# One addition of the last four variances to VectorE, and GpSimd's small operations of rows 8 to 13 in the order of rows

## The chip, the cores and the metric

The kernel runs on one core of a Trainium2 chip. The metric is the device time of one execution in microseconds (us): the median of several runs. The core's engines are named as the profile names them: PE (TensorE), DVE (VectorE), ACT (ScalarE), POOL (GpSimd) and SP (SyncE).

## The reference

Two blocks follow each other, each with a residual connection, on `x` of 2048 tokens by 448 channels. The first is a long convolution that is gated by the normalised input; the second is an MLP that mixes the tokens.

```python
def _layernorm(x, axis=-1, eps=1e-5):
    m = jnp.mean(x, axis=axis, keepdims=True)
    v = jnp.var(x, axis=axis, keepdims=True)
    return (x - m) / jnp.sqrt(v + eps)
...
    h = x + _A_ref(_layernorm(x, axis=-1), A_k, A_v, A_shift_k, A_ssm_k, A_ssm_D)   # q * (causal conv of kv + kv * D)
    h2 = h + _B_ref(_layernorm(h, axis=-1), B_w1, B_b1, B_w2, B_b2)
...
    u = _gelu(jnp.einsum("bsd,sf->bdf", h, w1) + b1)      # inside _B_ref, h normalised
    y = jnp.einsum("bdf,fs->bds", u, w2) + b2
```

## The kernel before, in words

The 2048 tokens lie as 128 partitions times 16 rows (token = 16 * partition + row). "Row r" below is one tile of 128 partitions by 448 channels. The convolution is done by a transform in two stages each way (`k1`, `k2`, `u1`, `u2`, products and `i1`, and at last `i2`); then the MLP's first matmuls (`mlp`) sum over the 16 rows.

**The stretch around the change** is the end of the convolution and the beginning of the MLP. For each row r:

- PE makes two matmuls for the row (line 1310) in a PSUM bank.
- From row 4 on, ACT (line 1320) or DVE (line 1322, rows 4, 14 and 15) reads the bank, scales it by the row's `qs[:, r, 3]` (one over the deviation of x's row) and adds 1. This is called the gate here.
- DVE multiplies with `x - mean` (line 1330 for rows 4 to 15), which gives the row of `h`, and leaves the row's sum in an accumulator. This is called the combination.
- ACT squares the row (line 1358) and accumulates the sum of squares.
- For each pair of rows POOL makes mean, square of the mean, variance, variance plus epsilon, and the power of -0.5: lines 1368, 1371, 1373, 1378 and 1382, five small operations on 128x2 numbers.
- DVE writes the normalised row into `Q` (line 1389). This is called the norm.
- PE multiplies row r of `Q` with row r of the first seven blocks of `w1` (line 1436, seven matmuls for a row, `mlp.r`).

**Statistics of x** are made before that, by DVE with `bn_stats` and `bn_aggr` (lines 1238 and 1240), and POOL adds epsilon (line 1246) and takes the power (line 1249) for four rows at once. For the last four, rows 12 to 15, these two are the steps `q.8:4` (the addition) and `q.8:5` (the power). The last aggregate that they need is `q.7:1`, of row 12.

**The order of work** on each engine is written out by hand in `ORDER`, a list of steps for each engine; an engine does its list strictly in order, and waits by semaphores for what other engines, or its own earlier instructions, have made. The steps that the text speaks of, by rows:

| rows | line 1368 | 1371 | 1373 | 1378 | 1382 (power) | norms on DVE |
|---|---|---|---|---|---|---|
| 4, 5 | i2.36:0 | i2.36:1 | i2.36:2 | i2.37 | i2.38 | i2.39, i2.40 |
| 6, 7 | i2.49:0 | i2.49:1 | i2.49:2 | i2.50 | i2.51 | i2.52, i2.53 |
| 8, 9 | i2.62:0 | i2.62:1 | i2.62:2 | i2.63 | i2.64 | i2.65, i2.66 |
| 10, 11 | i2.75:0 | i2.75:1 | i2.75:2 | i2.76 | i2.77 | i2.78, i2.79 |
| 12, 13 | i2.88:0 | i2.88:1 | i2.88:2 | i2.89 | i2.90 | i2.91, i2.92 |

DVE's list around the change: `q.7:1` (aggregate of row 12), norm of row 4, combination of 8, norm of 5, combinations of 9 and 10, norms of 6 and 7, combinations of 11, 13 and 12, norms of 8 and 9, gate of 14, norms of 10 and 11, combination of 14, gate of 15. PE's list: ... `mlp.7`, then parts of `mlp.8` to `mlp.11` mixed: the first matmul after `mlp.7` needs row 8 of `Q`, the fifth row 9, the eleventh row 10; then come the two matmuls of row 15 (line 1310), and then the first that needs row 11.

Of the kernel before, what the change touches and what calls it, by code (L numbers as in the profile page):

```python
# [80 lines left out]
    ),  # L81
# [118 lines left out]
class _Sched:  # L200
# [50 lines left out]
    def op(self, W, fn, r=(), w=(), br=(), bw=(), n=0, kind=None, est=None, dmab=None, keng=16, rate=None, after=(), safter=(), mode=0):  # L251
        if (self.tag, self.t0) != self.step:
            self.step = (self.tag, self.t0)
            self.count[self.tag] = self.count.get(self.tag, -1) + 1
        o = _Op()
        o.id = len(self.ops)
        o.engs = W if isinstance(W, tuple) else (W,)
        o.eng = None
        o.fn = fn
        o.is_dma = dmab is not None  # L260
        o.nbytes = dmab or 0
        o.keng = keng
        o.lat = 2000.0 + o.nbytes / (22.0 * keng) if o.is_dma else 0.0
        if o.is_dma:
            o.est = {e: (585.0 if e == "pool" else 700.0 if keng <= 8 else 460.0) for e in o.engs}
        elif est is not None:
            o.est = dict(est) if isinstance(est, dict) else {e: est for e in o.engs}
        else:
            o.est = {e: self.est_of(e, n, kind) for e in o.engs}
        o.ev = None  # L270
        o.mode = mode
        o.step = "%s.%d" % (self.tag, self.count[self.tag])
        o.rate = rate or (208.0 if keng == 8 else 425.0)
        o.tag = self.tag
        o.acq = []
        o.bufs = []
        o.extra = []
        preds = set(after)
        spreds = set(safter)
        for spec in r:  # L280
            for c in self._cells(spec):
                preds.update(c.w)
                c.r.append(o.id)
        for spec in w:
            g = spec[2] if len(spec) > 2 else None
            for c in self._cells(spec):
                rd = [x for x in c.r if x != o.id]
                if g is not None and c.g == g and not rd:
                    preds.update(c.gb)
                    c.w.append(o.id)  # L290
                else:
                    base = rd if rd else list(c.w)
                    preds.update(base)
                    c.w = [o.id]
                    c.r = []
                    c.g = g
                    c.gb = base
        for b in br:
            if len(self.ops) and all(self.ops[x].engs == ("pe",) for x in b.writers):
                preds.add(b.writers[-1])  # L300
            else:
                preds.update(b.writers)
            b.readers.append(o.id)
            o.bufs.append(b)
            b.users.append(o.id)
        for b in bw:
            if not b.writers:
                o.acq.append(b)
            else:
                spreds.add(b.writers[-1])  # L310
            b.writers.append(o.id)
            o.bufs.append(b)
            b.users.append(o.id)
        preds.discard(o.id)
        spreds -= preds
        o.preds = sorted(preds)
        o.spreds = sorted(spreds)
        self.ops.append(o)
        return o.id
# [259 lines left out]
def _build(nc, A_q, A_k, A_v, A_shift_k, A_ssm_k, A_ssm_D, B_w1, B_b1, B_w2, B_b2, out):  # L579
# [54 lines left out]
    with ctx:  # L634
        sch = _Sched(nc, ctx, n_dma_sems=112, small_off=SMALL)
        op = sch.op
# [5 lines left out]
        def view(off, shape, dtype=bf16):  # L642
            size = 4 if dtype in (f32, i32) else 2
            n = 1
            for s_ in shape:
                n *= s_
            ap = AR[:, off // 2: off // 2 + n * size // 2]
            if dtype is not bf16:
                ap = ap.bitcast(dtype)
            if len(shape) == 2:  # L650
                ap = ap.rearrange("p (a b) -> p a b", b=shape[1])
            elif len(shape) == 3:
                ap = ap.rearrange("p (a b c) -> p a b c", b=shape[1], c=shape[2])
            return ap
# [48 lines left out]
        def small(nb):  # L703
            o = sm["o"]
            sm["o"] = o + nb
            assert sm["o"] <= TOT
            return o
# [511 lines left out]
        o_qst = small(16 * 16)  # L1219
# [7 lines left out]
        def emit_q():  # L1227
            op("pool", lambda e, W: e.memset(cst[:, 0:2], -0.5), w=[(o_c2, 16, "c")])
            op("pool", lambda e, W: e.memset(cst[:, 2:3], 1.0), w=[(o_c2, 16, "c")])
            sch.t0 = T_Q  # L1230
            qs = view(o_qst, [R, 4], f32)
            for g in range(8):
                sch.t0 = T_Q + T_DQ * g
                for i in range(2):
                    r = 2 * g + i
                    ob = o_bst + 24 * (r % 4)
                    bs = view(ob, [6], f32)
                    op("dve", lambda e, W, bs=bs, r=r: e.bn_stats(out=bs, in_=XR(r)), r=[(oX(r), DB)],  # L1238
                       w=[(ob, 24)], n=D, kind="1x")
                    op("dve", lambda e, W, bs=bs, r=r: e.bn_aggr(out=qs[:, r, 0:2], in_=bs), r=[(ob, 24)],  # L1240
                       w=[(o_qst + 16 * r, 8)], n=6)
                if g >= 2 and g % 2 == 0:
                    continue
                r0, nr = (2 * g, 2) if g < 2 else (2 * g - 2, 4)
                rs = [(o_qst + 16 * (r0 + i), 16) for i in range(nr)]
                op("pool", lambda e, W, r0=r0, nr=nr: e.tensor_scalar(
                    out=qs[:, r0:r0 + nr, 2], in0=qs[:, r0:r0 + nr, 1], scalar1=EPS, scalar2=None, op0=ALU.add),
                   est=500.0, r=rs, w=[(o_qst + 16 * (r0 + i) + 8, 4) for i in range(nr)])
                op("pool", lambda e, W, r0=r0, nr=nr: e.tensor_tensor(
                    out=qs[:, r0:r0 + nr, 3], in0=qs[:, r0:r0 + nr, 2], in1=cst[:, 0:1].broadcast_to([128, nr]), op=ALU.pow),  # L1250
                   est=1000.0, r=rs + [(o_c2, 16)], w=[(o_qst + 16 * (r0 + i) + 12, 4) for i in range(nr)])
# [178 lines left out]
        def emit_mlp():  # L1430
# [21 lines left out]
            for r in range(R):  # L1452
# [23 lines left out]
                ("k1", emit_stage1, (KT, o_KT, TK, o_TK, "k")), ("k2", emit_stage2, (TK, o_TK, 1.0 / 2048.0)),  # L1476
                ("u1", emit_stage1, (V, o_V, TU, o_TU, "u")),  
                ("xload", emit_xload, ()), ("bias", emit_bias, ()), ("q", emit_q, ()),
                ("u2", emit_stage2, (TU, o_TU, None)), ("ew", emit_ew, ()), ("i1", emit_products_i1, ()), ("ct", emit_ct, (True,)), ("xn", emit_xn, ()), ("w1a", emit_w1_load, (0,)),
                ("warm", emit_warm, (N_WZ, T_I2 - 50.0, lambda: i1_last[-1:])),  # L1480
# [40 lines left out]
```

## Time and profile before

| | before |
|---|---|
| median of 3 runs | 172.8 us (172.39 to 172.85) |
| the profiled execution | 172.45 us, of which the profile's span is 170.3 us |
| PE busy | 160.4 us, 94% of the span |
| DVE busy | 104.0 us, 61% |
| ACT busy | 88.4 us, 52% |
| POOL busy | 61.2 us, 36% |
| granted clock of PE | 1.0 in this execution |

Times in the rows of the trace count from the start of the span. In a row of the timeline the columns are the start, the duration, the engine, the line and operation, and in brackets the idle time of the engine before it with what ended it. On DVE and PE the recorded duration of an instruction reaches somewhat beyond the start of the next one, since they are pipelined.

### The profile page before, as it was taken

To read this page: it belongs to the slowest core of one execution; us is meant where nothing else is said; L and a number is where in the kernel's file an instruction comes from. 1 tells how busy PE (TensorE), PEld (TensorE's weight loads), DVE (VectorE), ACT (ScalarE), POOL (GpSimd) and SP (SyncE) were. 2 spreads that over 40 slices of the span, in tenths; PEclk is the share of its full clock that TensorE was granted. 3 is DMA by queue.
4 is the path that set the end of the run, shared out by engine and by line. 5 is a ranking of instruction groups with operands and counts; after the bars stand their busy time and mean duration, and the time that the engine had idled before them with its cause. 6 is when DMAs were issued, how large, how long until landed. Compare 5 with 4: busy or idle time off the path is not lost.

```text
span 170.3 us, 3575 instructions
## 1 busy us (share of the span) xinstructions
PE 160.4 (94%) x1419; PEld 93.5 (55%) x1419; DVE 104.0 (61%) x192; ACT 88.4 (52%) x128; POOL 61.2 (36%) x156
## 2 busy tenths in 40 slices
PE   6999999899988899969998999999999999999994
PEld 2786756324333343524554555555567777777783
DVE  7998998999999999999977730000003223132231
ACT  3597859779989999998976143102360000000000
POOL 8346727482870554685888540000000000000000
PEclk9999999999999999999999999999999999999999
DMA  5999898775648875657999999930000111101111
GB/s 163 416 304 383 276 293 344 283 287 192 211 118 295 284 208 156 188 171 250 390 394 402 422 421 422 416 127 0 0 0 4 54 54 54 54 0 58 54 54 54
DMA packets 15564, 35.15 MB, mean 206 GB/s; under 512 B 3804, under 2 KB 9644, under 8 KB 15548
## 3 DMA queue, kind: packets, MB, share of 16 engines
q1 hardware_dynamic: 12396, 28.26, 45.6%
q0 software_dynamic: 3008, 6.58, 12.0%
q8 instruction: 11, 0.18, 0.4%
q10 hardware_dynamic: 144, 0.08, 0.2%
q14 instruction: 5, 0.04, 0.1%
HBM read 22.05 MB, written 1.84 MB: 140 GB/s over the span
## 4 chain that ended last, share of the span: by engine, by line
PE 60%; DVE 12%; ACT 11%; POOL 7%; DMA 6%; issue 3%; DVEq 0%; POOLq 0%; ACTq 0%
PE ps L1458 25%; PE ps L1446 12%; ACT arena L739 7%; PE ps L1436 6%; DMA arena<-arena 6%; PE ps L1025 3%; PE ps L966 3%; DVE arena L1161 3%; PE ps L1178 2%; PE ps L1038 2%; ACT arena L1069 2%; PE ps L1059 2%; DVE arena L1007 2%; POOL arena L1075 2%; DVE arena L1340 2%
## 5 line engine op out<-in xcount | busy, mean ns | idle before, releaser
L1461 DVE SCALAR_TENSOR_TENSOR arena<-ps,arena 128x448 bf16<-128x448 f32 (+2 forms) x17 | 11.1, 656 | 55.9 <-PE ps L1458 55.9
L1458 PE MATMUL ps<-arena 128*128 128x448 bf16 (+2 forms) x238 | 42.7, 342 | 0.0
L1458 PEld LDWEIGHTS ps<-arena 128*128 128x128 bf16 x238 | 33.3, 145 | 9.5
L1436 PE MATMUL ps<-arena 128*128 128x448 bf16 x112 | 23.8, 353 | 0.6 <-DVE arena L1389 0.6
L739 ACT CAST arena<-ps 128x896 bf16<-128x896 f32 (+1 forms) x29 | 23.3, 897 | 0.7 <-PE ps L1178 0.4
L1069 ACT CAST arena<-ps 128x896 bf16<-128x896 f32 x24 | 20.3, 915 | 5.2 <-PE ps L1059 5.2
L1446 PE MATMUL ps<-arena 128*128 128x448 bf16 x112 | 22.5, 352 | 0.0
L1075 POOL DMA_DIRECT2D arena<-arena x32 | 17.6, 555 | 12.9 <-ACT arena L1069 12.8
L1426 ACT ACTIVATE arena<-ps,arena 128x448 bf16<-128x448 f32 x14 | 7.9, 642 | 18.2 <-PE ps L1436 10.6
L1436 PEld LDWEIGHTS ps<-arena 128*128 128x128 bf16 x112 | 10.7, 98 | 11.4 <-DVE arena L1389 1.7
L1161 DVE TENSOR_TENSOR arena<-arena 128x1792 bf16<-128x1792 bf16 x16 | 16.6, 1080 | 0.2
L1446 PEld LDWEIGHTS ps<-arena 128*128 128x128 bf16 x112 | 11.0, 98 | 10.2
L1059 PE MATMUL ps<-arena 128*32 128x448 bf16 x256 | 15.0, 355 | 1.7 <-ACT arena L1069 0.5
L1094 PE MATMUL ps<-arena 128*64 128x448 bf16 x128 | 15.3, 360 | 1.0 <-ACT arena L740 0.4
L1178 PE MATMUL ps<-arena 64*128 64x448 bf16 x128 | 14.2, 351 | 1.4 <-ACT arena L739 0.6
L1202 POOL DMA_DIRECT2D arena<-arena x16 | 9.3, 587 | 12.7 <-ACT arena L739 12.7
L1358 ACT ACTIVATE arena<-arena 128x448 bf16<-128x448 f32 x14 | 8.0, 573 | 6.3 <-DVE arena L1330 6.2
L1094 PEld LDWEIGHTS ps<-arena 128*64 128x64 f16 x128 | 5.5, 108 | 10.1 <-ACT arena L739 2.8
L1178 PEld LDWEIGHTS ps<-arena 64*128 64x128 f16 x128 | 5.3, 94 | 9.6 <-DVE arena L1161 3.5
L1059 PEld LDWEIGHTS ps<-arena 128*32 128x32 f16 x256 | 5.4, 95 | 9.2 <-ACT arena L1069 2.1
L1389 DVE TENSOR_SCALAR arena<-arena 128x448 bf16<-128x448 f32 x16 | 7.8, 510 | 4.0 <-POOL arena L1382 4.0
L1238 DVE BATCH_NORM_STATS2 arena<-arena 128x6 f32<-128x448 bf16 x16 | 9.6, 609 | 0.0
(97 smaller groups left out, 193.7 us busy)
## 6 DMA issues: line engine op xcount, KB each, us to landing
arena<-in_B_w_dram SPq DMA_DIRECT2D x8, 896.0 KB, 10.1
arena<-in_B_w_dram SPq DMA_DIRECT2D x2, 2048.0 KB, 17.1
arena<-arena SPq DMA_DIRECT2D x16, 224.0 KB, 3.7
arena<-arena POOLq DMA_DIRECT2D x32, 112.0 KB, 3.8
arena<-in_B_w_dram SPq DMA_DIRECT2D x2, 1536.0 KB, 19.0
arena<-arena POOLq DMA_DIRECT2D x13, 196.0 KB, 4.1
arena<-in_A_k_dram SPq DMA_DIRECT2D x4, 448.0 KB, 5.9
arena<-in_A_v_dram SPq DMA_DIRECT2D x4, 448.0 KB, 9.1
```

The costliest lines, as they stand in the source:

```text
L739: return e.copy(out=dst(), in_=src())
L1059: op("pe", lambda e, W, b=b, r=r, q=q, x=x, c0=c0: e.matmul(PS[32 * q:32 * q + 32, b.slots[x], 0:D], E[:, 2 * r + x, c0:c0 + 32], src[:, r ...
L1069: return e.copy(out=dst, in_=Ppair(b)) if W == "act" else e.tensor_copy(out=dst, in_=Ppair(b))
L1075: shuf[tag].append(op(q_, lambda e, W, g=g, i=i, a=a, nu=nu, jh=jh: e.dma_start(T[a + i:a + i + 4 * nu - 3:4].rearrange("p (j k) c d -> p ...
L1094: op("pe", lambda e, W, b=bs[h], h=h, j=j, c=c, par=par: e.matmul(PS[64 * par:64 * par + 64, b.slots[c], 0:D], FW[:, 64 * c:64 * c + 64], ...
L1161: op("dve", lambda e, W, m=m, i=i: e.tensor_tensor(out=MR(m.slots[0]).rearrange("p (x y) d -> p x y d", x=2), in0=TU[:, i].unsqueeze(2).br ...
L1178: k = op("pe", lambda e, W, b=bs[h], m=ms[h], par=par, t=t, tab=tab, xy=xy, P=P: e.matmul(Pb(b, par), tab[P, :], MR(m.slots[0])[P, xy, :], ...
L1238: op("dve", lambda e, W, bs=bs, r=r: e.bn_stats(out=bs, in_=XR(r)), r=[(oX(r), DB)], w=[(ob, 24)], n=D, kind="1x")
L1436: op("pe", lambda e, W, r=r, fc=fc, b=bs[fc]: e.matmul(Pb(b), W1A[:, r, 128 * fc:128 * fc + 128], Q[:, r, :], start=(r == 0), stop=(r == R ...
L1446: op("pe", lambda e, W, r=r, fc=fc, b=b: e.matmul(Pb(b), W1B[:, r, 128 * (fc - n0):128 * (fc - n0) + 128], Q[:, r, :], start=(r == 0), sto ...
L1458: op("pe", lambda e, W, r=r, fc=fc, b=b, d0=d0, d1=d1: e.matmul(Pb(b)[:, d0:d1], W2[fc // 7][:, fc % 7, r:S:R], G[:, fc, d0:d1], start=(fc ...
L1461: op("dve", lambda e, W, r=r, b=b, A=A, d0=d0, d1=d1: e.scalar_tensor_tensor(out=XR(r)[:, d0:d1], in0=Pb(b)[:, d0:d1], scalar=bm[:, r:r + ...
```

## The change

The addition `q.8:4` (line 1246, 128x4 numbers of rows 12 to 15) is done by DVE, right after the aggregate `q.7:1` that it needs and ahead of the norm of row 4; POOL had done it between the powers `i2.38` and `q.8:5`. In POOL's list the operations of rows 8 to 13 stand in the order of rows: the power of rows 8 and 9 (`i2.64`) comes ahead of the first two operations of rows 10 and 11 (`i2.75:0`, `i2.75:1`), and the first one of rows 12 and 13 (`i2.88:0`) behind the power of rows 10 and 11 (`i2.77`). The sum of the means and the bias (`i2.0`, line 1287) stays ahead of `i2.89`. Nothing else moves.

```diff
 "dve":
-        "i2.29:0 i2.16:0 i2.30:0 i2.47:0 i2.26:0 i2.43:0 q.7:0 q.7:3 i2.27:0 q.7:1 i2.39:0 i2.56:0 i2.40:0 "
+        "i2.29:0 i2.16:0 i2.30:0 i2.47:0 i2.26:0 i2.43:0 q.7:0 q.7:3 i2.27:0 q.7:1 q.8:4 i2.39:0 i2.56:0 i2.40:0 "
 "pool":
-        "q.8:4 q.8:5 i2.49:1 i2.49:2 i2.50:0 i2.51:0 i2.62:0 i2.62:1 i2.62:2 i2.63:0 i2.75:0 i2.75:1 i2.64:0 "
-        "i2.75:2 i2.88:0 i2.76:0 i2.77:0 i2.88:1 i2.88:2 i2.0:0 i2.89:0 i2.90:0 i2.101:0 i2.101:1 i2.101:2 "
-        "i2.102:0 i2.103:0 "
+        "q.8:5 i2.49:1 i2.49:2 i2.50:0 i2.51:0 i2.62:0 i2.62:1 i2.62:2 i2.63:0 i2.64:0 i2.75:0 i2.75:1 i2.75:2 "
+        "i2.76:0 i2.77:0 i2.88:0 i2.88:1 i2.88:2 i2.0:0 i2.89:0 i2.90:0 i2.101:0 i2.101:1 i2.101:2 i2.102:0 "
+        "i2.103:0 "
 emit_q:
-                op("pool", lambda e, W, r0=r0, nr=nr: e.tensor_scalar(
+                op("dve" if g == 7 else "pool", lambda e, W, r0=r0, nr=nr: e.tensor_scalar(
                     out=qs[:, r0:r0 + nr, 2], in0=qs[:, r0:r0 + nr, 1], scalar1=EPS, scalar2=None, op0=ALU.add),
-                   est=500.0, r=rs, w=[(o_qst + 16 * (r0 + i) + 8, 4) for i in range(nr)])
+                   est=92.0 if g == 7 else 500.0, r=rs, w=[(o_qst + 16 * (r0 + i) + 8, 4) for i in range(nr)])
```

## The prediction, made before the result was known

> **What bounds the kernel now.** I first read the page for the span, then the chain of waits, which lies on PE for most of its length but passes through POOL and DVE ahead of one PE matmul, and then the timelines of PE, POOL and DVE for that stretch.
>
> ```profile
> span 170.3 us, 3575 instructions
> ```
> ```profile
> 92.35 0.58 DVE arena L1389
> 92.93 0.05 issue
> 92.97 3.01 PE ps L1436 x15
> ```
> ```profile
> 91.03 1.49 PE L1436 MATMUL ps<-arena 128*128 128x448 bf16 x7
> 92.97 2.82 PE L1436 MATMUL ps<-arena 128*128 128x448 bf16 x14 [0.45 <-DVE arena L1389]
> ```
> ```profile
> 92.97:125.30 32.33, 32.33 (x171) 1.00 0.60 247
> 125.30:167.39 42.09, 42.09 (x235) 1.00 0.11 42
> ```
>
> The profiled execution took 172.45 us, 2.15 beside its span; the median of the three runs is 172.8. The last two rows (stretch, PE busy, matmuls, clock) say that PE has no gap after 92.97: whatever PE gains there, the end gains too. They also give a matmul each 32.33 / 171 = 0.189 us. After `mlp.7`'s seven matmuls from 91.03 the next was due at 91.03 + 7 x 0.189 = 92.35. It came at 92.97, since the norm of row 8 ended at 92.93. So PE lost **0.62 us**, and that is all the change can win. The rest of the working asks when rows 8 and 10 of `Q` are ready.
>
> **POOL sets the norm of row 8.** Its timeline has each of its operations in the order of the list, from `q.8:4` (84.77) to the power of rows 10 and 11 (93.04):
>
> ```profile
> 84.77 0.51 POOL L1246 TENSOR_SCALAR arena<-arena 128x4 f32<-128x4 f32 x1
> 85.36 1.37 POOL L1249 TENSOR_TENSOR arena<-arena 128x4 f32<-128x4 f32 x1
> 86.70 0.21 POOL L1371 TENSOR_TENSOR arena<-arena 128x2 f32<-128x2 f32 x1
> 86.99 0.53 POOL L1373 TENSOR_TENSOR arena<-arena 128x2 f32<-128x2 f32 x1
> 87.61 0.19 POOL L1378 TENSOR_SCALAR arena<-arena 128x2 f32<-128x2 f32 x1
> 87.88 0.70 POOL L1382 TENSOR_TENSOR arena<-arena 128x2 f32<-128x2 f32 x1
> 88.66 0.50 POOL L1368 TENSOR_SCALAR arena<-arena 128x2 f32<-128x2 f32 x1
> 89.25 0.35 POOL L1371 TENSOR_TENSOR arena<-arena 128x2 f32<-128x2 f32 x1
> 89.68 0.52 POOL L1373 TENSOR_TENSOR arena<-arena 128x2 f32<-128x2 f32 x1
> 90.29 0.19 POOL L1378 TENSOR_SCALAR arena<-arena 128x2 f32<-128x2 f32 x1
> 90.56 0.49 POOL L1368 TENSOR_SCALAR arena<-arena 128x2 f32<-128x2 f32 x1
> 91.14 0.50 POOL L1371 TENSOR_TENSOR arena<-arena 128x2 f32<-128x2 f32 x1
> 91.59 0.72 POOL L1382 TENSOR_TENSOR arena<-arena 128x2 f32<-128x2 f32 x1
> 92.29 0.19 POOL L1373 TENSOR_TENSOR arena<-arena 128x2 f32<-128x2 f32 x1
> 92.45 0.22 POOL L1368 TENSOR_SCALAR arena<-arena 128x2 f32<-128x2 f32 x1
> 92.75 0.21 POOL L1378 TENSOR_SCALAR arena<-arena 128x2 f32<-128x2 f32 x1
> 93.04 0.87 POOL L1382 TENSOR_TENSOR arena<-arena 128x2 f32<-128x2 f32 x1
> ```
> ```profile
> 84.33 0.17 DVE L1240 BATCH_NORM_AGGREGATE arena<-arena 128x2 f32<-128x6 f32 x1
> 84.72 0.51 DVE L1389 TENSOR_SCALAR arena<-arena 128x448 bf16<-128x448 f32 x1 [0.23 <-POOL arena L1382]
> 85.15 0.68 DVE L1330 SCALAR_TENSOR_TENSOR arena<-arena 128x448 f32<-128x448 bf16 x1
> ...
> 86.18 0.68 DVE L1330 SCALAR_TENSOR_TENSOR arena<-arena 128x448 f32<-128x448 bf16 x1
> 86.78 0.08 DVE L1330 DVE_READ_ACCUMULATOR arena<-arena 128x1 f32 x1
> 86.78 0.68 DVE L1330 SCALAR_TENSOR_TENSOR arena<-arena 128x448 f32<-128x448 bf16 x1
> ...
> 90.29 0.69 DVE L1330 SCALAR_TENSOR_TENSOR arena<-arena 128x448 f32<-128x448 bf16 x1
> 90.90 0.08 DVE L1330 DVE_READ_ACCUMULATOR arena<-arena 128x1 f32 x1
> 90.90 0.68 DVE L1330 SCALAR_TENSOR_TENSOR arena<-arena 128x448 f32<-128x448 bf16 x1
> ```
>
> Two things are to be seen. POOL never rests here; an operation that waits for the one before it starts 0.08 after that one's end. And the same small operation costs 0.19 to 0.22 or about 0.5. The long ones end 0.05 to 0.07 after a norm or combination of DVE: the addition at 85.28 (norm to 85.23), the one from 86.99 at 87.52 (combination to 87.46), the one from 91.14 at 91.64 (combination to 91.58). The one at 90.29, which starts together with a combination, still takes 0.19. So **an operation of POOL that comes in the middle of such an instruction waits for its end**, and then needs about 0.05 beyond the recorded one; powers too: the one of 85.36 ends at 86.73, 0.90 after the combination that it met (to 85.83). This makes POOL's times no plain sum.
>
> The Trainium skill has a rule for this: GPSIMD Engine Reference, Specifications, says that GpSimd shares its interfaces to SBUF with VectorE, with contention from VectorE instructions in a two-port mode or with two SBUF inputs. By it, the durations of moved operations don't move with them, and the new addition on VectorE, which reads SBUF alone, could itself hold POOL up; the rows above agree for norms and combinations, and none shows it for an addition of four columns.
>
> **The addition on DVE.** It reads what the aggregate just ahead of it writes, so DVE waits for its own result. The nearest rows for such a wait are the last aggregates of an earlier stage:
>
> ```profile
> 72.25 0.59 DVE L1238 BATCH_NORM_STATS2 arena<-arena 128x6 f32<-128x448 bf16 x1
> ```
> ```profile
> 72.87 0.18 DVE L1240 BATCH_NORM_AGGREGATE arena<-arena 128x2 f32<-128x6 f32 x1
> ```
>
> The aggregate starts at 72.87, 0.03 after its statistics ended (72.84). Here the aggregate ends at 84.50, so the addition starts at about 84.53, and with 0.17 (the aggregate's duration; the addition is no larger) ends at 84.70. The norm of row 4, queued behind it, starts only at 84.72, for it waits for POOL's power: DVE has been idle for 0.23. So I cost the addition at nothing on DVE. If that cover is gone, the norm of row 4 and the four instructions behind it slip by the difference. The bounds are a gain of nothing and a loss of 0.17.
>
> **POOL without it.** `q.8:5` starts at 84.77, in the addition's place (its input is there at 84.70), meets the norm of row 4 (to 85.23) and ends 0.90 after that: 86.13, not 86.73. The gain of 0.60 is not kept. `i2.49:1` (0.21) ends at about 86.31; `i2.49:2`, due at 86.39, meets the combination of row 9 (86.18 to 86.86) and ends at 86.91; `i2.50`, due at 86.99, meets that of row 10 (to 87.46): 87.52; the power `i2.51` starts at 87.60 and ends at 88.30 in place of 88.58. **0.28 is left.** DVE's next norms wait for this power, and the three operations of rows 8 and 9 run beside them as now, so `i2.63` starts 90.29 - 88.58 = 1.71 after it, at 90.01, and ends at 90.20.
>
> **The order of rows.** `i2.64` now follows at once, at 90.28, where before it stood behind two operations of 0.49 and 0.50. The combination of row 13 starts at 90.29, as before, since it waits for ACT's gate. As with the row of 90.29, POOL's operation comes in time and takes its 0.72: it ends at 91.00, not 92.31. The norm of row 8 then waits for nothing but DVE, which has two combinations to finish (the second starts at 90.90 and lasts as long as the first, 0.61 to the next start): it runs from 91.53 to about 92.11, and with 0.05 more PE has row 8 at 92.16, ahead of 92.35. **The 0.62 goes.**
>
> **What is late next** is row 10, eleventh after `mlp.7`: due at 92.35 + 10 x 0.189 = 94.24. POOL's `i2.75:0` starts at 91.08 and meets the combination of row 12: 91.63. `i2.75:1` meets the norm of row 8: about 92.1. `i2.75:2` meets that of row 9: about 92.5. Then DVE has the gate of row 14, which reads PSUM. The nearest rows for that are these:
>
> ```profile
> 79.95 0.68 DVE L1322 TENSOR_SCALAR arena<-ps,arena 128x448 f32<-128x448 f32 x1
> ```
> ```profile
> 80.36 0.20 POOL L1373 TENSOR_TENSOR arena<-arena 128x2 f32<-128x2 f32 x1 [0.29 <-ACT arena L1358]
> ```
>
> POOL's operation took 0.20 in the midst of a gate, so a gate blocks nothing. `i2.76` then runs from 92.6 to 92.8 and the power `i2.77` from 92.88 to 93.60, 0.3 earlier than now (93.91); the norm of row 10 takes 0.51 to 0.58 and ends at 94.12 to 94.2, just in time. I take 0.02 as lost there. The first operation of rows 12 and 13 moves from 92.45 behind that power; their norms are needed a row and more later on PE.
>
> **Sum**: 172.45 - 0.62 + 0.02 = 171.85 against the profiled execution, which stood 0.35 below the median; against the median **172.2 us**.
>
> **Rivals.**
>
> *A, half of it.* `i2.64` at 90.28 comes some hundredths too late and has to wait for the combination of row 13 to end (90.90). It then ends at about 91.55. Row 8 is still in time (norm 91.59 to 92.17), but `i2.75:0` now meets the norm of row 8 and `:1` that of row 9 (92.6); the power `i2.77` ends at 93.95, the norm of row 10 at 94.5, 0.3 late. Gain 0.3: 172.5. For it: 0.01 us decides by my times. Against it: the row of 90.29 did slip in.
>
> *B, nothing.* The addition costs DVE or POOL 0.15 to 0.28 after all, the power of rows 6 and 7 stays near 88.58, and the stall moves from row 8 to row 10: 172.8. For it: the page's rule would let the addition hold up POOL for its 0.17. Against it: POOL then still calculates the power before.
>
> *C, slower.* In the order of rows, rows 10 and 11 pay for rows 8 and 9. If `i2.51` ends later than 88.58 (the point from which this decides; the addition and its wait would have to push the norm of row 4 by 0.28), `i2.63` misses the start of the combination and ends at 90.95 or later, `i2.64` meets the next one and ends at 92.16; `i2.75:0` and `:1` then meet both norms (93.2), `i2.77` ends at 94.54 and row 10 comes at 95.15, where PE now has it at 92.97 + 10 x 0.189 = 94.86: 0.3 slower, 173.1. Were gates to block too, 0.5 more, 173.6. Against it: DVE's idle 0.23, and POOL's 0.20 within a gate.
>
> **Chances.** Forecast 0.55, A 0.18, B 0.07, C 0.20. About 0.3% (0.52 us) can be told from no change when this kernel is measured. The forecast's 0.60 lies over it (0.54 faster, 0.01 taken off as too near); A, B, that 0.01 and 0.08 of C lie within: 0.34; the rest of C, with some other price of the same kind that I can't see, is slower: 0.12. The range reaches from the whole 0.62 with the 0.4 by which the lowest run stands under the median (171.8) to C (173.1); the forecast's own is 171.8 to 172.4.
>
> **What would show it.** Right: line 1246 has one row on DVE near 84.53, and the norm of row 4 still starts at 84.72; the power of rows 6 and 7 ends near 88.3, that of rows 8 and 9 near 91.0, with no long row between; PE's matmul after `mlp.7` shows no idle time before it, and PE is full to the end. A shows as idle time of PE eleven matmuls later; C as a power of rows 8 and 9 beyond 91.6 and one of rows 10 and 11 beyond 94. I am wrong if PE waits anywhere after 92.35 for the norm of a row by more than 0.1.

## The result, and the profile after

The changed kernel takes 171.78 us (median of 8 runs, 171.46 to 172.62), the kernel before 172.82 beside it (8 runs, 172.37 to 173.35). The ratio is **0.9946, with a 95% interval of 0.9919 to 0.9972**: faster by 0.3 to 0.8%, or 0.5 to 1.4 us. The forecast was 172.2 us, with 0.62 us gained at one stall of PE; 171.78 lies at the very lower end of its range (171.8). All ratios and means here leave out two executions with a lower granted clock (0.99), one of the kernel before and one in the experiments.

The profiled execution took 171.71 us, with a span of 169.7 (before: 172.45 and 170.3). In its chain of waits (start, duration, what) POOL and DVE are gone from the stretch between 80 us and the last matmul; it lies on PE alone there, and the matmuls behind `mlp.7` come without a gap:

```profile
90.85 0.38 PE ps L1310 x2
91.23 4.16 PE ps L1436 x22
95.39 0.38 PE ps L1310 x2
```

Before, the 22 were 7 and 15 with 0.62 between them. The busy time of PE in the stretches that follow has no gap either:

```profile
91.06:125.00 33.94, 33.94 (x181) 1.00 0.64 259
124.55:166.99 42.44, 42.44 (x238) 1.00 0.11 41
```

POOL's timeline, from the power of x's last variances (`q.8:5`, 84.77) to that of rows 10 and 11 (92.60):

```profile
84.77 1.01 POOL L1249 TENSOR_TENSOR arena<-arena 128x4 f32<-128x4 f32 x1
85.74 0.20 POOL L1371 TENSOR_TENSOR arena<-arena 128x2 f32<-128x2 f32 x1
86.02 0.28 POOL L1373 TENSOR_TENSOR arena<-arena 128x2 f32<-128x2 f32 x1
86.38 0.50 POOL L1378 TENSOR_SCALAR arena<-arena 128x2 f32<-128x2 f32 x1
86.97 1.04 POOL L1382 TENSOR_TENSOR arena<-arena 128x2 f32<-128x2 f32 x1
88.09 0.22 POOL L1368 TENSOR_SCALAR arena<-arena 128x2 f32<-128x2 f32 x1
88.39 0.21 POOL L1371 TENSOR_TENSOR arena<-arena 128x2 f32<-128x2 f32 x1
88.69 0.34 POOL L1373 TENSOR_TENSOR arena<-arena 128x2 f32<-128x2 f32 x1
89.11 0.51 POOL L1378 TENSOR_SCALAR arena<-arena 128x2 f32<-128x2 f32 x1
89.70 0.72 POOL L1382 TENSOR_TENSOR arena<-arena 128x2 f32<-128x2 f32 x1
90.50 0.58 POOL L1368 TENSOR_SCALAR arena<-arena 128x2 f32<-128x2 f32 x1
91.17 0.50 POOL L1371 TENSOR_TENSOR arena<-arena 128x2 f32<-128x2 f32 x1
91.75 0.35 POOL L1373 TENSOR_TENSOR arena<-arena 128x2 f32<-128x2 f32 x1
92.19 0.33 POOL L1378 TENSOR_SCALAR arena<-arena 128x2 f32<-128x2 f32 x1
92.60 0.72 POOL L1382 TENSOR_TENSOR arena<-arena 128x2 f32<-128x2 f32 x1
```

The power of rows 6 and 7 ends at 88.01 (88.58 before), that of rows 8 and 9 at 90.42 (92.31), that of rows 10 and 11 at 93.32 (93.91). DVE's timeline has the addition, and the norms of rows 8 and 9 without a wait ahead of them:

```profile
84.30 0.17 DVE L1240 BATCH_NORM_AGGREGATE arena<-arena 128x2 f32<-128x6 f32 x1
84.50 0.18 DVE L1246 TENSOR_SCALAR arena<-arena 128x4 f32<-128x4 f32 x1
84.69 0.52 DVE L1389 TENSOR_SCALAR arena<-arena 128x448 bf16<-128x448 f32 x1
...
91.54 0.93 DVE L1389 TENSOR_SCALAR arena<-arena 128x448 bf16<-128x448 f32 x2
92.39 0.68 DVE L1322 TENSOR_SCALAR arena<-ps,arena 128x448 f32<-128x448 f32 x1
93.36 0.94 DVE L1389 TENSOR_SCALAR arena<-arena 128x448 bf16<-128x448 f32 x2 [0.30 <-POOL arena L1382]
```

The addition starts 0.03 after its aggregate's end and lasts 0.18; the norm of row 4 starts at 84.69, no later than before (84.72), since the addition fits into what was idle time.

### The profile page after: what moved, and what is told of

The parts are those of the page before. It is cut to its first block, busy times and chain, and to the rows that moved or that the text cites. A ratio compares the mean times of both kernels' runs of the same rounds, so it can differ in the third digit from the quotient of the medians.

```text
span 169.7 us, 3575 instructions
## 1 busy us (share of the span) xinstructions
PE 159.8 (94%) x1419; PEld 93.5 (55%) x1419; DVE 104.1 (61%) x193; ACT 88.4 (52%) x128; POOL 60.4 (36%) x155
## 4 chain that ended last, share of the span: by engine, by line
PE 68%; ACT 13%; DMA 8%; POOL 4%; DVE 3%; issue 2%; DVEq 0%; ACTq 0%; POOLq 0%
PE ps L1458 25%; PE ps L1436 13%; PE ps L1446 12%; ACT arena L739 8%; DMA arena<-arena 8%; PE ps L1025 3%; POOL arena L1075 3%; ACT arena L1069 3%; PE ps L966 3%; PE ps L1310 3%; PE ps L1059 3%; PE ps L1038 3%; ACT arena L740 2%; PE ps L992 2%; PE ps L1178 2%
## 5 line engine op out<-in xcount | busy, mean ns | idle before, releaser
L1436 PE MATMUL ps<-arena 128*128 128x448 bf16 x112 | 23.7, 353 | 0.1
L1436 PEld LDWEIGHTS ps<-arena 128*128 128x128 bf16 x112 | 10.8, 98 | 10.6 <-DVE arena L1389 0.7
```

The lines of the kernel that those rows point to most:

```text
L1436: op("pe", lambda e, W, r=r, fc=fc, b=bs[fc]: e.matmul(Pb(b), W1A[:, r, 128 * fc:128 * fc + 128], Q[:, r, :], start=(r == 0), stop=(r == R ...
```

## The experiments

**How they are read.** Where PE's part of the MLP begins differs by up to 1.6 us from one execution to the next, for reasons that lie ahead of it (79.16 to 80.71 among all profiles). That widens the intervals of the ratios. The profiles allow a closer measure: the time from the start of the first L1436 matmul to the start of the last matmul of all. In the kernel before it is 88.10 (167.59 - 79.49), in the changed one 87.53 (166.99 - 79.46). The difference, 0.57, is the stall of 0.62 less 0.05 that PE loses in some profiles (those with 87.53 in place of 87.47) within 1.8 us after the first L1436 matmul, ahead of everything that the change moves.

| kernel | first L1436 to last matmul | PE's loss behind `mlp.7` | end of the powers of rows 6/7, 8/9, 10/11, after the first L1436 matmul | ratio to before, 95% |
|---|---|---|---|---|
| before | 88.10 | 0.62 | 9.09, 12.83, 14.43 | |
| before_again | 87.95 | 0.46 | 9.09, 12.68, 14.28 | 0.9992 [0.9969, 1.0016] |
| before_third | 88.10 | 0.62 | 9.10, 12.83, 14.44 | |
| before_fourth | 87.96 | 0.47 | 9.10, 12.68, 14.29 | |
| after | 87.53 | none | 8.54, 10.96, 13.86 | 0.9946 [0.9919, 0.9972] |
| after_again | 87.53 | none | 8.54, 10.96, 13.86 | 0.9954 [0.9934, 0.9974] |
| add_only | 87.47 | none | 8.54, 11.40, 13.81 | 0.9940 [0.9919, 0.9961] |
| order_only | 87.53 | none | 9.10, 11.53, 14.13 | 0.9968 [0.9942, 0.9995] |
| before_late | 88.10 | 0.61 | 9.09, 12.83, 14.43 | 1.0004 [0.9975, 1.0033] |
| order_late | 87.56 | 0.03, at row 10 | 9.09, 12.13, 14.23 | 0.9972 [0.9946, 0.9999] |
| dve_twice | 87.53 | none | 8.65, 11.06, 13.86 | 0.9967 [0.9938, 0.9996] |
| no_power | 87.47 | none | 8.57, 10.99, 13.82 | 0.9962 [0.9934, 0.9990] |
| before_far | 88.44 | 0.12 at row 6, 0.82 at row 8 | 9.36, 13.17, 14.77 | 1.0016 [0.9982, 1.0050] |
| order_far | 88.17 | 0.08 at row 6, 0.33 at row 8, 0.21 at row 10 | 9.38, 12.74, 14.85 | 0.9985 [0.9946, 1.0025] |

before_third and before_fourth are one execution each and have no ratio.

**The two kernels once more.** No edit. Expected of the kernel before:

> The kernel before, unchanged, to see how much its stall varies from one execution to the next. If the stall at row 8 is the whole of the difference (theory 1), PE loses 0.5 to 1.0 us behind mlp.7 here too and is full after it; the ratio to itself holds 1.000. If the measured gain of about 0.9 us comes partly from elsewhere (theory 2), the stall is again near 0.6 and the span differs from 170.3 by waits in other stages.

> The kernel before, once more, for one more profile: if the stall is the whole of the change's gain, PE loses about 0.45 to 0.65 behind mlp.7 here too; a loss over 0.8 would say that the kernel before often loses more than its two profiles show, as the measured ratios near 0.995 suggest.

> As before_third, a fourth profile of the kernel before: a stall of 0.45 to 0.65, or over 0.8 if the kernel before often loses more than the first two profiles show.

and of the changed one:

> The changed kernel, unchanged. Theory 1: no idle time of PE behind mlp.7, ratio 0.9964 (0.62 of 172.8) or lower by as much as the stall of the kernel before is larger in other executions. Theory 2: 0.9946 again, with waits of other stages shorter than in the kernel before.

The stall has two sizes, 0.62 and 0.46, each in two of four profiles. In before_again POOL's operations of rows 8 and 9 were shorter, and the power of rows 8 and 9 met a combination instead (1.18 in place of 0.72). The first of these operations, that power, and PE's matmuls behind the stall in before_again:

```profile
88.33 0.23 POOL L1368 TENSOR_SCALAR arena<-arena 128x2 f32<-128x2 f32 x1
90.66 1.18 POOL L1382 TENSOR_TENSOR arena<-arena 128x2 f32<-128x2 f32 x1
92.49 3.01 PE L1436 MATMUL ps<-arena 128*128 128x448 bf16 x15 [0.30 <-DVE arena L1389]
```

So theory 1 held for the stall's existence, and the lower bound of its range, 0.5, was a little high. A loss over 0.8, by which the stall alone would explain a ratio near 0.9946, was seen in none. The changed kernel again has no stall, and 0.9954. No other stage was shorter in the profiles: the first L1436 matmul comes at 79.16 to 80.38 in the four of the kernel before, at 79.46 and 80.07 in the two of the changed one, and from the last matmul to the end of the span it is 2.7 us in all six. What theory 2 has right lies outside the span; the section on the prediction comes to it.

**The addition alone**, POOL's list otherwise as before:

```diff
 "pool" (against the changed kernel)
-        "q.8:5 i2.49:1 i2.49:2 ... i2.63:0 i2.64:0 i2.75:0 i2.75:1 i2.75:2 i2.76:0 i2.77:0 i2.88:0 i2.88:1 "
+        "q.8:5 i2.49:1 i2.49:2 ... i2.63:0 i2.75:0 i2.75:1 i2.64:0 i2.75:2 i2.88:0 i2.76:0 i2.77:0 i2.88:1 "
```

> The addition on VectorE alone; GpSimd's list otherwise as before (the power of rows 8 and 9 behind the first two operations of rows 10 and 11). Theory 1 (an operation of GpSimd waits for the end of a norm or combination that it meets): the power of rows 6 and 7 ends near 88.0 as in the changed kernel, the first two operations of rows 10 and 11 fall into VectorE's pause before 90.3 and cost 0.2 each, the power of rows 8 and 9 ends near 90.9 to 91.6, and PE has no stall: the whole 0.6 us. Rival (GpSimd's times add up as they stood before): the power of rows 8 and 9 ends 0.59 earlier than 92.31, at 91.72, the norm of row 8 at 92.3, PE loses 0.0 to 0.1, also nearly the whole gain; the rival has the two operations at 0.5 each.

The stall is gone, as both theories had it. What tells them apart are the two operations of rows 10 and 11, 90.32 and 90.62 in POOL's timeline of this kernel, just ahead of the power of rows 8 and 9:

```profile
90.32 0.22 POOL L1368 TENSOR_SCALAR arena<-arena 128x2 f32<-128x2 f32 x1
90.62 0.19 POOL L1371 TENSOR_TENSOR arena<-arena 128x2 f32<-128x2 f32 x1
90.77 0.72 POOL L1382 TENSOR_TENSOR arena<-arena 128x2 f32<-128x2 f32 x1
```

They had cost 0.49 and 0.50 in the kernel before, where combinations ran; here they fall into DVE's pause. Times on POOL don't add up as they stood.

**The order alone**, the addition on POOL:

```diff
 "pool" (against the changed kernel)
-        "q.8:5 i2.49:1 i2.49:2 i2.50:0 ... "
+        "q.8:4 q.8:5 i2.49:1 i2.49:2 i2.50:0 ... "
```

> The order of rows alone; the addition stays on GpSimd. Theory 1: the power of rows 6 and 7 ends at 88.58 as before; the power of rows 8 and 9, due at 90.56, meets the combination of row 13 and ends near 91.55; the norm of row 8 is in time, but the two operations of rows 10 and 11 meet the norms of rows 8 and 9, their power ends near 93.95 and PE stalls for 0.3 us eleven matmuls later: gain 0.3 us, ratio 0.998. Rival (times add up): the power of rows 8 and 9 ends 1.0 earlier, at 91.3, rows 10 and 11 as before at 93.9, due 94.24: norm ends at 94.45, also a stall of 0.2 to 0.3; it differs by having the power at 0.72 unblocked. Second rival (the order alone brings the whole gain): no stall, 0.62.

Here theory 1, as I had worked it out, was wrong: no stall at all. The power of rows 6 and 7 ended 9.10 after the first matmul, as before; but behind it the operations were short, and the power of rows 8 and 9 came ahead of the combination of row 13 (90.45) and was not held up:

```profile
88.77 0.23 POOL L1368 TENSOR_SCALAR arena<-arena 128x2 f32<-128x2 f32 x1
89.08 0.21 POOL L1371 TENSOR_TENSOR arena<-arena 128x2 f32<-128x2 f32 x1
89.36 0.35 POOL L1373 TENSOR_TENSOR arena<-arena 128x2 f32<-128x2 f32 x1
89.80 0.51 POOL L1378 TENSOR_SCALAR arena<-arena 128x2 f32<-128x2 f32 x1
90.39 0.73 POOL L1382 TENSOR_TENSOR arena<-arena 128x2 f32<-128x2 f32 x1
```

So **each half of the change takes the whole stall away by itself**, in one profile each; for the order, order_late below shows a second one, with long operations, and 0.03 lost. Together the halves bring the power of rows 8 and 9 sooner than either alone (10.96 after the first matmul, not 11.40 or 11.53), which PE doesn't need.

**More work on POOL**, one more addition behind `q.8:4` (`q.8:6`, into unused numbers), in the old order and in the order of rows:

```diff
 emit_q (before_late, and the same in order_late), "pool": "q.8:4 q.8:6 q.8:5 ..."
+                if g == 7: op("pool", lambda e, W: e.tensor_scalar(out=qx[:, 8:12, 0], in0=qs[:, 12:16, 1], scalar1=EPS, scalar2=None, op0=ALU.add), ...)
```

> The kernel before with one more small addition (128x4) on GpSimd behind the addition that the change moves, so that GpSimd's work for rows 6 to 13 comes later. Theory 1 (GpSimd's operations wait out the norms and combinations that they meet): the power of rows 6 and 7 ends not 0.6 but 0.2 to 0.4 later, since some of the waits are the same ones; the power of rows 8 and 9, behind two operations of rows 10 and 11, ends 14.0 to 14.8 after the first L1436 matmul (12.7 and 12.8 in the two profiles of the kernel before); PE loses 0.7 to 1.3 us behind mlp.7 (0.46 and 0.62 there). Rival (times add up): 0.6 later all along, the stall grows by 0.6 to 1.1 or 1.2.

> The same one more addition on GpSimd, with the order of rows. Rival C of the prediction (in the order of rows, rows 10 and 11 pay for rows 8 and 9 as soon as GpSimd is late): the norm of row 8 comes 0 to 0.5 late, the power of rows 10 and 11 ends 14.5 to 15.1 after the first L1436 matmul and PE stalls a second time eleven matmuls later, 0.3 to 0.9 in all, as much as or more than the kernel before. Theory 1 without that: one stall of at most 0.3 and less loss than the same lateness in the old order.

The additional operation cost nothing. In POOL's timeline of before_late it starts while the addition ahead of it is still held up by a norm, and both are done when `q.8:5` can start:

```profile
85.26 0.51 POOL L1246 TENSOR_SCALAR arena<-arena 128x4 f32<-128x4 f32 x1
85.47 0.34 POOL L1252 TENSOR_SCALAR arena<-arena 128x4 f32<-128x4 f32 x1
85.86 1.36 POOL L1249 TENSOR_TENSOR arena<-arena 128x4 f32<-128x4 f32 x1
```

The powers then end at the very times, to 0.01, that they have in the kernel before. The theory of sums is out (it had 0.6 later), and theory 1's 0.2 to 0.4 was too much. The two kernels do share the lateness of the power of rows 6 and 7 (9.09), and differ in the order alone: 0.61 lost at row 8 in the old one, 0.03 in the order of rows. These 0.03 lie at row 10, where rival C has its loss, but are a tenth of the least that C had.

**More lateness still**, a power in place of the additional addition:

```diff
 emit_q (before_far, and the same in order_far)
-                if g == 7: op("pool", lambda e, W: e.tensor_scalar(out=qx[:, 8:12, 0], in0=qs[:, 12:16, 1], ...
+                if g == 7: op("pool", lambda e, W: e.tensor_tensor(out=qx[:, 8:12, 0], in0=qs[:, 12:16, 1], in1=cst[:, 0:1].broadcast_to([128, 4]), op=ALU.pow), ...
```

> The kernel before with one more power (128x4, about 1.0 us) on GpSimd behind the addition that the change moves: a lateness that no wait can hide whole. Theory 1: the power of rows 6 and 7 ends 0.75 to 1.3 later, so row 6 is late for PE by 0.5 to 1.1, and row 8, behind the two operations of rows 10 and 11, by 1.1 to 1.9 in all: 88.6 to 89.4 us from the first L1436 matmul to the last (88.10 and 87.95 in the two profiles of the kernel before). Rival (the rest of the path has more slack than that): less than 88.5.

> The same one more power on GpSimd, with the order of rows. Theory 1: row 6 is late by the same 0.5 to 1.1; the power of rows 8 and 9 ends 0.5 or more earlier than in the old order, so the whole is 88.0 to 88.6. Rival C of the prediction (rows 10 and 11 pay): the stall at row 10 makes it as long as the old order with the same power.

Of a power that takes about 1.0 us where nothing holds it up (1.01 for `q.8:5` in the changed kernel), 0.27 to 0.28 arrives at rows 6 and 7 and 0.34 at rows 8 and 9 in the old order. Theory 1's 0.75 to 1.3 was wrong; with 88.44 the expectation's rival, more slack, was right. In the order of rows the mechanism of rival C does appear at last. PE's timeline of before_far, and then that of order_far:

```profile
93.68 3.01 PE L1436 MATMUL ps<-arena 128*128 128x448 bf16 x15 [0.66 <-DVE arena L1389]
```
```profile
94.06 3.23 PE L1436 MATMUL ps<-arena 128*128 128x448 bf16 x15 [0.17 <-DVE arena L1389]
```

The same 15 matmuls take 3.23 in place of 3.01 in order_far: the second stall, of 0.21, is at row 10, eleventh behind `mlp.7`. But row 8 comes 0.49 sooner (0.33 lost, not 0.82), and the whole is 0.27 shorter than in the old order.

**The price on DVE doubled**, a second addition that waits for the first:

```diff
 "dve": "... q.7:1 q.8:4 q.8:6 i2.39:0 ..."
+                if g == 7: op("dve", lambda e, W: e.tensor_scalar(out=qx[:, 8:12, 0], in0=qs[:, 12:16, 2], scalar1=EPS, scalar2=None, op0=ALU.add), ...)
```

> The changed kernel with a second addition on VectorE right behind the first, which waits for it: the price of the moved addition doubled. VectorE has no idle time left ahead of the norm of row 4, so this norm and the combinations behind it come 0.15 to 0.2 later. Theory 1: the power of rows 6 and 7 comes up to 0.2 later, row 8 is still in time, PE has no stall, 87.5 us from the first L1436 matmul to the last one, as in the changed kernel. Rival (VectorE's cover decides, B and C of the prediction): the delay reaches row 8 or 10 and PE loses 0.1 to 0.3.

87.53, no stall; the power of rows 6 and 7 ends 0.11 later than in the changed kernel, and that of rows 10 and 11 not at all. Twice the price is still hidden.

**Less work on POOL**, a multiplication in place of the power `q.8:5`:

```diff
-                op("pool", lambda e, W, r0=r0, nr=nr: e.tensor_tensor(
+                op("pool", lambda e, W, r0=r0, nr=nr, g=g: e.tensor_scalar(
+                    out=qs[:, r0:r0 + nr, 3], in0=qs[:, r0:r0 + nr, 2], scalar1=20.0, scalar2=None, op0=ALU.mult) if g == 7 else e.tensor_tensor(...
```

> The changed kernel, where the power of x's last four variances is left out (a multiplication by 20 stands in its place, so rows 12 to 15 are scaled wrongly); GpSimd has 0.5 to 0.8 us less to do ahead of row 8. Theory 1: PE is full from the first L1436 matmul on in the changed kernel, so nothing more is gained: 87.5 us from the first L1436 matmul to the last. Rival (GpSimd still bounds this stretch): up to 0.5 us more.

87.47, as add_only: nothing more is gained. Here are the operations of this kernel from the multiplication to the power of rows 6 and 7:

```profile
85.03 0.48 POOL L1249 TENSOR_SCALAR arena<-arena 128x4 f32<-128x4 f32 x1
85.58 0.52 POOL L1371 TENSOR_TENSOR arena<-arena 128x2 f32<-128x2 f32 x1
86.18 0.36 POOL L1373 TENSOR_TENSOR arena<-arena 128x2 f32<-128x2 f32 x1
86.63 0.51 POOL L1378 TENSOR_SCALAR arena<-arena 128x2 f32<-128x2 f32 x1
87.22 1.06 POOL L1382 TENSOR_TENSOR arena<-arena 128x2 f32<-128x2 f32 x1
```

POOL saved 0.53 on the first of them (1.01 to 0.48) and lost it again by the third: the next ones now meet other instructions of DVE (0.52 and 0.36 in place of 0.20 and 0.28), and the power ends 8.57 after the first matmul, in the changed kernel 8.54.

## Why the prediction was right, and where its steps were off

*What bounds it.* Right for what lies in the span. PE lost 0.62 behind `mlp.7` for the norm of row 8 and had no other stall from there to its last matmul, and with it gone the time from the first L1436 matmul to the last is 0.57 shorter (0.42 in the executions with the smaller stall). By four profiles of the kernel before, the stall is 0.54 on average, 0.31% of 172.8. The seven measurements without it have ratios from 0.9940 to 0.9972, on average 0.9958, 0.72 us, so the stall is most of the gain.

*What lies outside the span.* Here the sum failed: it left the 2.15 us of the time that lie beside the span as they were, without a reason. Every run has its span on record (to 0.1 us) beside its time. The mean span is shorter than that of the kernel before, measured beside it, by 0.64 (after_again), 0.80 (add_only), 0.65 (order_only), 0.39 (order_late), 0.42 (dve_twice) and 0.40 (no_power), on average 0.55. Each of these is uncertain by 0.2 to 0.4, but their mean agrees with the stall. What the time has beside the span is on average

| kernels | time beside the span, us |
|---|---|
| before (three groups of runs), order_only | 2.17, 2.19 |
| after, after_again, add_only, dve_twice, no_power: the addition on DVE | 1.93 to 1.98 |
| before_late, order_late, before_far, order_far: one operation more on POOL | 2.05 |

So about 0.2 us of the changed kernel's gain lies outside the profiled span. The order alone (order_only) has none of it. But one operation more on POOL lowers the time beside the span too, by 0.12, so what decides it is open; the profiles don't show this time. With 0.54 + 0.21 the ratio would be 0.9957, which all five intervals with the addition on DVE hold; the stall alone, 0.9969, is in order_only's (0.9968).

*The addition on DVE.* Right: at 84.50 (forecast 84.53), 0.18 long (0.17), and the norm of row 4 not later. By dve_twice, PE doesn't lose even where the cover is overrun.

*POOL without it.* Right in sign, and forecast at half the size. I had `q.8:5` held up by the norm of row 4 until 86.13; it wasn't (1.01, end 85.78). The power of rows 6 and 7 ended 0.55 earlier, counted from the first L1436 matmul (8.54, not 9.09), where I had 0.28. The step that failed is the rule that an operation of POOL that comes in the middle of a norm waits for its end: the addition that had started 0.05 after a norm waited, the power that starts 0.08 after one doesn't. Nor does the distance alone decide: the multiplication that no_power has in this place, also 0.08 after the norm, was held up (0.48). The prediction's own rows had an exception too: line 1368 at 92.45 took 0.22 in the midst of the norm of row 8 (92.35 to 92.93).

*The order of rows.* Right in its result, wrong in how near it was: the power of rows 8 and 9 ended at 90.42, 0.58 sooner than forecast. Half of that came with the power of rows 6 and 7; the other half from the operations of rows 8 and 9, of which three took 0.22, 0.21 and 0.34, not 0.50, 0.35 and 0.52, while the fourth met the combination of row 11 and took 0.51, not 0.19. That the errors fell on the good side is luck: in order_late the power did meet the combination of row 13 (1.06). The norms of rows 8 and 9 started at 91.54 (forecast 91.53), because DVE, not POOL, sets that time.

*What is late next.* The power of rows 10 and 11 ended at 93.32 (forecast 93.60), and row 10 was in time; the 0.02 that I had taken off weren't lost.

*The rivals.* A's condition, that the power of rows 8 and 9 misses the combination's start, didn't occur in the changed kernel; where it did (order_late, 1.06 long), the loss was 0.03, not 0.3, since the operations of rows 10 and 11 were short behind it. B is refuted by the 88.01 of the power of rows 6 and 7 and by dve_twice. The new addition didn't hold POOL up either: the power that POOL ran beside it, of 83.94, took 0.72, as without it (83.97 in the kernel before), and in dve_twice the power that starts 0.05 into the second addition took 1.01, as in the changed kernel. C has the right mechanism, but it took a power of rows 6 and 7 later by 0.28 than in order_only to see 0.21 of stall at row 10, and the old order loses more at row 8 then; C itself had 0.3 slower than before. With that one power more the order of rows is 0.07 longer than the kernel before (88.17 and 88.10), and still shorter than the old order with the same power (88.44). My expectation of order_only failed by the same term as the order of rows above: it rested on durations (0.50, 0.35, 0.52) of one profile, and the next ones had 0.23, 0.21 and 0.35.

## What to carry to other kernels

Where a small engine's chain feeds the big one, look for the one wait that PE really has, and ask what is queued ahead of it: here either taking one half-microsecond operation out of the queue or letting the row that is due first go first was enough, and the second remedy for the same stall brought PE nothing more. Durations of small operations that contend with another engine are no constants to be added: work out which instruction each one meets, give each outcome both prices, and don't trust a forecast that hangs on hundredths of a microsecond. When runs scatter by more than the effect, measure in the trace between two events that enclose the change and exclude the scatter; and compare what the time has beside the span as well, since such a measure can't see it.

## What the runs showed of the hardware that was not expected

One and the same operation, 128x2 on POOL right after the power of rows 6 and 7, and started 0.05 after a norm, took 0.50 in the kernel before and 0.22 in the changed one (88.66 and 88.09; the norms from 88.62 and 88.04), and 0.23 in before_again. The two sizes of the stall, 0.62 and 0.46, go with it (0.50 in before_third too, 0.23 in before_fourth too). What decides was not found; it is finer than the 0.01 us of the rows, and it wasn't tried to take the contention away, for which the norms would have to be done by another engine.

Two independent operations of POOL overlap: an addition that is held up by DVE hides the next one nearly whole (85.26 to 85.77 and 85.47 to 85.81 in before_late). So an operation less on POOL can be worth half a microsecond or nothing, by what it stands beside: without the addition the power of rows 6 and 7 came 0.55 sooner, before_late's additional one was free, and no_power's saved 0.53 was lost within three operations.
